# Loading the first batch's keys and queries of a head pair into one tile, keys on even and queries on odd partitions

## The chip, the core and the metric

The kernel runs on one core of a Trainium2 chip. The metric is the device time of one launch in microseconds (us), taken as the median over runs. The core has a matrix engine (PE), two elementwise engines (DVE, and ACT, which also computes the exponential), a general engine (POOL), a sequencer that mainly issues transfers (SP), and 16 DMA engines that carry all transfers between HBM and the on-chip memory.

## The reference

Attention over four batches of eight heads, and then a feed-forward layer with the maximum of three products. Heads 0, 2 and 6 see all earlier positions; the other five see the first four positions and a window of 64.

```python
scores = scale * np.matmul(q, k.transpose(0, 1, 3, 2))      # B=4, H=8, S=768, D=64
causal = rel >= 0
stream_keep = causal & (is_sink | in_win)                   # n_sink=4, window=64
scores = np.where(mask, scores, -1e9)                       # mask: causal or stream_keep, by head
a = softmax(scores)
x = np.matmul(a, v)                                         # -> rows of B*S=3072 by H*D=512
h = np.maximum(np.maximum(x @ w1, x @ w2), x @ w3)          # 512 -> 768
out = h @ w_out                                             # 768 -> 512, float32
```

Inputs are float32; the kernel computes in float16 with float32 sums.

## The kernel before

One table, `PROGRAM`, sets the order of all work: each word such as `cast 0 1 pd` calls one helper, which issues its instructions on fixed engines. Each engine runs its own instructions in that order and waits on semaphores. So nothing overtakes anything on one engine, and a late operand holds up all that stands behind it there.

Batch 0 has a path of its own, in halves of 384 positions (`HALF`), and the heads in four pairs, (0,2), (1,3), (4,6), (5,7). For each half and pair there are these steps:

- `hl half hp n ..` (`load_pairs`, DMA issues on line 206) brings the float32 keys and queries of `n` pairs from HBM. Keys go to a tile `ks`, queries to a tile `qs`, 128 partitions each. Partition p holds three consecutive rows of each head (`HB` = 3), 768 bytes that lie together in HBM. A packet is one such run. The two letters name the issuing queues for keys and queries (s is SP, c is ACT). There are 16 such loads of 192 KB in batch 0, 3.1 MB in all.
- `cast half hp ..` (`cast_pair`, line 220) makes float16 tiles `kn` and `qn`, one cast for the keys and one for the queries, each on the engine that its letter names (d DVE, a ACT, p POOL, r DVE by a reduction).
- `turnp half hp ..` (`turn_pair`, lines 238 and 241) transposes on PE into PSUM (`tr`), three 128x128 transposes for the keys and three for the queries, and copies the result into `KQ`, which holds keys and queries with the head dimension on partitions. With two letters, keys and queries are copied by two instructions, keys by the first letter's engine.
- `kx0` (lines 561 and 566) copies from the keys of `KQ` what a windowed head needs of the far block into `kx`; `s0` (lines 596, 611, 632) computes scores on PE into `st` and the exponential on ACT into `pt`.

The values come by `load_v` (line 298 in batch 0, also 768-byte runs), are cast on POOL (`vc`, line 500) and put in order by a product with a 0/1 matrix (`vt`, lines 508 and 513). From batch 1 on, keys and queries come by casting transfers that POOL issues (`load`, line 261, tile `kq`) and are turned by DVE (line 275). POOL also issues the casting loads of the weights (`w`, line 401: `w0t`, `w1t`, `w2t`). `f` is the product with a weight (line 440), `av` the product of scores and values (line 720).

The tiles of the first two loads, `ks0`, `qs0`, `ks1` and `qs1`, stand alone. The other three groups (`n` = 2, two pairs in a tile) share two buffers of the pool `pairs2`, so the third group waits until the casts have read the first. A transfer also waits for the one that last used its semaphore; eight semaphores (DMAHW0 to 7) go round among the loads of SP and ACT.

Of the kernel before, what the change touches and what calls it, by code (L numbers as in the profile page):

```python
# [9 lines left out]
FP16 = mybir.dt.float16  # L10
FP32 = mybir.dt.float32
# [5 lines left out]
PAIRS = ((0, 2), (1, 3), (4, 6), (5, 7))  # L17
# [136 lines left out]
def fast(ctx, tc, keep, q, k, v, is_retrieval, n_sink, window, moe_w1, moe_w2, moe_w3, moe_w_out, w_t, woutt, out):  # L154
    nc = tc.nc
    B, H, S, D = q.shape
    DMdl = out.shape[1]
    DF = moe_w1.shape[1]
    P = 128
# [4 lines left out]
    HALF = S // 2  # L164
    HB = HALF // P
# [9 lines left out]
    pairs2 = ctx.enter_context(tc.tile_pool(name="pairs2", bufs=2))  # L175
    once = ctx.enter_context(tc.tile_pool(name="once", bufs=1))
    third = ctx.enter_context(tc.tile_pool(name="third", bufs=2))
    half16 = ctx.enter_context(tc.tile_pool(name="half16", bufs=3))
# [11 lines left out]
    def bank(shape, dtype, name):  # L190
        return bkp.tile(shape, dtype, tag="bank", name=name)
# [4 lines left out]
    staged, cast, KQs, landed = {}, {}, {}, {}  # L196

    def load_pairs(half, hp, n, engines):
        for nm, src, eng in zip(("ks", "qs"), (k, q), engines):
            st = (  # L200
                pairs2.tile([P, 4, HB, D], FP32, tag=nm, name=nm) if n == 2
                else once.tile([P, 2 * n, HB, D], FP32, name=f"{nm}{hp}")
            )
            for h in range(0, 2 * n, 2):
                h0, h1 = PAIRS[hp + h // 2]
                eng.dma_start(
                    out=st[:, h : h + 2],
                    in_=src[0, h0 : h1 + 1 : h1 - h0, half * HALF : (half + 1) * HALF].rearrange(
                        "h (p j) d -> p h j d", p=P
                    ),  # L210
                )
            for i in range(n):
                staged.setdefault((half, hp + i), []).append(st[:, 2 * i : 2 * i + 2])
                landed[half, hp + i] = st[0:1, 2 * i, 0, 0:2]

    def cast_pair(half, hp, engines):
        cast[half, hp] = []
        for nm, src, op in zip(("kn", "qn"), staged.pop((half, hp)), engines):
            x = half16.tile([P, HB, 2, D], FP16, tag=nm, name=nm)
            op(out=x, in_=src.rearrange("p h j d -> p j h d"))  # L220
            cast[half, hp].append(x)

    def of_pair(hp):
        return KQs[0, hp // 2].rearrange("p i t two -> p i (t two)")[
            :, hp % 2
        ].rearrange("p (i t) -> p i t", i=2)

    def turn_pair(half, hp, *engines):
        if (0, hp // 2) not in KQs:
            KQs[0, hp // 2] = qkt.tile([P, 2, S, 2], FP16, tag="KQ", name="KQ")  # L230
        xs = cast.pop((half, hp))
        n = 2 // len(engines)
        for part, op in enumerate(engines):
            tr = bank([P, 1024], FP16, "tr")
            for i in range(n):
                for j in range(HB):
                    c = i * HALF + j * P
                    nc.tensor.transpose(
                        tr[:, c : c + P], xs[part + i][:, j].rearrange("p h d -> p (h d)"), ident
                    )  # L240
            op(
                out=of_pair(hp)[
                    :, part : part + n, half * HALF : (half + 1) * HALF
                ].rearrange("p i (t j) -> p i t j", j=HB),
                in_=tr[:, 0 : n * HALF].rearrange("p (i j t) -> p i t j", i=n, j=HB),
            )

    def load(b, quad, *which):
# [61 lines left out]
    def load_first(half, hp, n, e="sc"):  # L310
        by = {"s": nc.sync, "c": nc.scalar}
        load_pairs(half, hp, n, [by[x] for x in e])
# [11 lines left out]
    def idle_work(n):  # L324
# [11 lines left out]
        out=kb[:, 2:4], in_=kb[:, 2:4], compare_op=ALU.is_ge, fill=0.0,  # L336
# [3 lines left out]
        out=kb[:, 3], in_=kb[:, 3], compare_op=ALU.is_gt, fill=0.0,  # L340
# [3 lines left out]
        out=kb[:, 1:5:3], in_=kb[:, 1:5:3], compare_op=ALU.is_gt, fill=0.0,  # L344
# [7 lines left out]
        out=every3, in_=every3, compare_op=ALU.not_equal, fill=1.0,  # L352
# [4 lines left out]
    if n_sink > 0:  # L357
# [4 lines left out]
        out=far, in0=kb[:, 0:5], scalar1=FAR, scalar2=-FAR, op0=ALU.mult, op1=ALU.add  # L362
# [74 lines left out]
    def hidden(b, half, wi, ni, op=None):  # L437
        yy = psum(b, half)
        for ks in range(KS):
            nc.tensor.matmul(  # L440
                yy[:, 0:HALF],
                w_t[wi][:, ks, ni * P : (ni + 1) * P],
                xT[b, half, ks].rearrange("p a t -> p (a t)"),
                start=(ks == 0), stop=(ks == KS - 1),
            )
        if wi == 0:
            acc[b, half, ni] = accp.tile([P, HALF], FP16, tag="acc", name="acc")
            op(out=acc[b, half, ni], in_=yy[:, 0:HALF])  # L448
            return
        if wi == 2:  # L450
            hT[b, half, ni] = htp.tile([P, HALF], FP16, tag=f"hT{ni}", name=f"hT{ni}")
        nc.vector.tensor_tensor(  # L452
            out=acc[b, half, ni] if wi == 1 else hT[b, half, ni],
            in0=yy[:, 0:HALF], in1=acc[b, half, ni], op=ALU.max,
        )
# [243 lines left out]
    def masks(b, s, xy, i, engine):  # L699
        rows, (c0, step), pattern = KEEP[s][xy][i]  # L700
        mask(pts[b, s, xy], rows[0], len(rows), c0, step, pattern, engine)
# [37 lines left out]
    def turn_x(b, half, hp, op):  # L739
        x = xs.pop((b, half, hp))  # L740
        tr = bank([P, 1024], FP16, "tr")
        for i in range(HB):
            nc.tensor.transpose(
                tr[:, i * P : (i + 1) * P], x[:, i].rearrange("p h d -> p (h d)"), ident
            )
        op(out=xT[b, half, hp].rearrange("p a t -> p (a t)"), in_=tr[:, 0:HALF])
# [55 lines left out]
    def reduce_one(out, in_):  # L802
# [5 lines left out]
    engines = {"d": nc.vector, "p": nc.gpsimd}  # L808
# [5 lines left out]
        k=lambda b, s, xy, i, e: masks(int(b), int(s), xy, int(i), engines[e]),  # L814
        f=lambda b, half, wi, ni, *e: hidden(int(b), int(half), int(wi), int(ni), *[ops[x] for x in e]),
# [7 lines left out]
        x=lambda b, half, hp, e: turn_x(int(b), int(half), int(hp), ops[e]),  # L823
        turn=lambda *a: turn(*map(int, a)),
        load=lambda *a: load(*map(int, a)),
        load_v=lambda b, half, *h: load_v(int(b), int(half), queues[h[-1]], *map(int, h[:-1])),
        hl=lambda h, hp, n, *e: load_first(int(h), int(hp), int(n), *e),
        cast=lambda h, hp, e: cast_pair(int(h), int(hp), [ops[x] for x in e]),
        turnp=lambda h, hp, e: turn_pair(int(h), int(hp), *[ops[x] for x in e]),
        idle=lambda n: idle_work(int(n)),  # L830
        clear=lambda j, e: clear_v(int(j), engines[e]),
# [213 lines left out]
```

## Time and profile before

| | us |
|---|---|
| median of three runs | 189.75 |
| lowest and highest run | 189.44, 190.21 |
| span of the profiled execution, first to last instruction | 188.2 |
| PE busy in it | 178.9 (95%) |
| DVE, ACT, POOL busy | 144.1, 99.4, 83.0 |
| batch 0's transfers from SP and ACT, in the main | 2 to 17 |
| POOL's casting loads of weights and batch 1 | 16 to 40 |

The profile gives the profiled execution as a span alone; the median of the runs lies 1.55 us above it, which is taken for what lies before the first and after the last instruction. Of the rows that follow, those of the timeline begin with the start in us and the duration in us; brackets at the end give how long the engine stood idle before and what released it. The chain of work goes back from the last instruction, at each step to what released it. The DMA views count packets, megabytes and the time the packets took, as a share of all 16 DMA engines' time; a share over 100% means that packets of an engine overlap. In the table of stages, the columns behind the engines' busy times are the granted clock of PE, the busy share of the DMA engines and the rate in GB/s.

### The profile page before, as it was taken

The page shows a single profiled execution, that of the slowest core. Times are in us where ns is not written, and L with a number is a line of the kernel's source. Part 1 is how long each engine was busy: PE and PEld are TensorE (multiplying, and loading weights), DVE is VectorE, ACT ScalarE, POOL GpSimd, SP SyncE. Part 2 cuts the span into 40 slices and gives each one's busy share as a digit, 9 for nine tenths or more (in the row PEclk, how much of TensorE's full clock was granted, in tenths as well). Part 3 has the DMA queues.
Part 4 walks back from the last instruction along what each step waited for, and adds up shares of the span by engine and source line. Part 5 has one row for each costly group of instructions (what it writes and reads, how often), then busy time and mean ns, then how long its engine had stood idle before and what let it go on. Part 6 is the DMA issues. An engine that isn't in the chain of part 4 may idle for free.

```text
span 188.2 us, 4755 instructions
## 1 busy us (share of the span) xinstructions
PE 178.9 (95%) x1863; PEld 105.4 (56%) x1863; DVE 144.1 (77%) x306; ACT 99.4 (53%) x161; POOL 83.0 (44%) x142
## 2 busy tenths in 40 slices
PE   7789898999999999999999999999999999999990
PEld 2355546566566456855555556655745574664550
DVE  3749997989899978888979899756874698574540
ACT  3399996368965648687096336764445301311110
POOL 7697899808884890199057002127213400000000
PEclk9999999999999999999999999999999999999999
DMA  5999999998799999439693301321231013301413
GB/s 172 325 329 275 213 212 208 212 229 188 163 130 158 144 280 185 127 74 236 156 262 80 112 0 56 66 80 56 41 87 74 0 62 69 129 0 56 167 56 120
DMA packets 43012, 26.30 MB, mean 140 GB/s; under 512 B 29802, under 2 KB 38506, under 8 KB 42986
## 3 DMA queue, kind: packets, MB, share of 16 engines
q1 hardware_dynamic: 37562, 17.24, 35.6%
q0 software_dynamic: 4192, 7.87, 23.4%
q10 hardware_dynamic: 1232, 0.85, 1.5%
q8 instruction: 15, 0.25, 0.6%
q14 instruction: 11, 0.09, 0.1%
HBM read 25.17 MB, written 6.29 MB: 167 GB/s over the span
## 4 chain that ended last, share of the span: by engine, by line
PE 78%; DMA 13%; DVE 2%; POOL 2%; ACT 2%; issue 1%; ACTq 0%; DVEq 0%; POOLq 0%
PE yy L440 44%; PE yy L465 15%; PE st L677 7%; PE oacc L720 7%; DMA kq<-in_k_dram 7%; DMA qs<-in_q_dram 5%; PE yst L440 3%; DVE KQ L275 2%; DMA ks<-in_k_dram 2%; PE yst L465 1%; DVE acc L452 1%; POOL vx L529 1%; ACT qn L220 0%; ACT pt L632 0%; POOL w1t L401 0%
## 5 line engine op out<-in xcount | busy, mean ns | idle before, releaser
L380 POOL TENSOR_TENSOR pt<-pt,kb 128x512 f16<-128x512 f16 (+5 forms) x53 | 48.3, 931 | 59.7 <-ACT pt L694 51.1
L694 ACT ACTIVATE pt<-st 128x1024 f16<-128x1024 f32 (+2 forms) x51 | 43.5, 908 | 25.1 <-PE st L677 24.7
L440 PE MATMUL yy<-xT,w2t 128*128 128x384 f16 x184 | 36.2, 326 | 0.0
L440 PE MATMUL yy<-xT,w0t 128*128 128x384 f16 x180 | 34.8, 326 | 0.0
L440 PE MATMUL yy<-xT,w1t 128*128 128x384 f16 x176 | 34.3, 326 | 0.0
L465 PE MATMUL yy<-woutt,hT 128*128 128x512 f16 (+1 forms) x138 | 31.4, 372 | 0.0
L452 DVE TENSOR_TENSOR hT<-yy,acc 128x384 f16<-128x384 f32 x46 | 25.2, 555 | 4.6 <-PE yy L440 2.9
L452 DVE TENSOR_TENSOR acc<-yy,acc 128x384 f16<-128x384 f32 x44 | 23.9, 554 | 6.2 <-PE yy L440 4.3
L275 DVE STREAM_TRANSPOSE KQ<-kq 128x384 f32<-128x384 f32 x24 | 25.5, 1131 | 1.3 <-DMA kq<-in_k_dram 1.1
L448 ACT CAST acc<-yy 128x384 f16<-128x384 f32 x27 | 12.9, 492 | 23.5 <-PE yy L440 21.4
L440 PEld LDWEIGHTS <-w0t 128*128 128x128 f16 x192 | 18.1, 98 | 12.8 <-issue 0.7
L440 PEld LDWEIGHTS <-w1t 128*128 128x128 f16 x192 | 17.8, 98 | 12.0 <-issue 0.6
L440 PEld LDWEIGHTS <-w2t 128*128 128x128 f16 x192 | 17.7, 98 | 11.8 <-issue 0.2
L465 PEld LDWEIGHTS <-hT 128*128 128x128 f16 x150 | 14.4, 98 | 15.3
L720 PEld LDWEIGHTS <-pt 128*128 128x128 f16 x472 | 17.2, 97 | 4.2 <-DVE pt L380 0.9
L720 PE MATMUL oacc<-va,pt 128*128 128x65 f16 x392 | 18.6, 193 | 0.8 <-DVE pt L380 0.8
L474 ACT COPY ot<-yy 128x512 f32<-128x512 f32 (+1 forms) x14 | 7.9, 565 | 21.5 <-PE yy L465 18.9
L727 DVE TENSOR_TENSOR x<-oacc,sums 128x384 f16<-128x384 f32 x32 | 17.8, 557 | 1.1
L632 ACT ACTIVATE pt<-st 128x1024 f16<-128x1024 f32 (+5 forms) x22 | 15.4, 769 | 0.4 <-PE st L611 0.2
L677 PE MATMUL st<-KQ 32*128 32x128 f16 (+2 forms) x342 | 15.2, 257 | 0.1
L380 DVE TENSOR_TENSOR pt<-pt,kb 128x256 f16<-128x256 f16 (+4 forms) x31 | 12.4, 405 | 2.1 <-ACT pt L694 2.1
L677 PEld LDWEIGHTS <-KQ 32*128 32x128 f16 x342 | 8.8, 92 | 6.8 <-issue 6.0
(117 smaller groups left out, 190.5 us busy)
## 6 DMA issues: line engine op xcount, KB each, us to landing
out_dram<-ot SPq DMA_DIRECT2D x23, 256.0 KB, 2.0
vs<-in_v_dram SPq DMA_DIRECT2D x18, 256.0 KB, 4.6
ks<-in_k_dram SPq DMA_DIRECT2D x8, 192.0 KB, 3.7
kq<-in_k_dram POOLq DMA_DIRECT2D x3, 384.0 KB, 8.1
kq<-in_q_dram POOLq DMA_DIRECT2D x3, 384.0 KB, 9.6
kq<-in_k_dram POOLq DMA_DIRECT2D x3, 288.0 KB, 5.7
kq<-in_q_dram POOLq DMA_DIRECT2D x3, 288.0 KB, 7.5
qs<-in_q_dram ACTq DMA_DIRECT2D x4, 192.0 KB, 4.9
```

The costliest lines, as they stand in the source:

```text
L275: nc.vector.transpose(out=dst.rearrange("c (p j) -> c j p", j=n)[:, j0:j1], in_=src.rearrange("c (j i) -> c j i", i=R),)
L380: engine.tensor_tensor(out=x, in0=x, in1=of_blocks(kb, pattern, rows), op=ALU.mult)
L440: nc.tensor.matmul(yy[:, 0:HALF], w_t[wi][:, ks, ni * P : (ni + 1) * P], xT[b, half, ks].rearrange("p a t -> p (a t)"), start=(ks == 0), s ...
L448: op(out=acc[b, half, ni], in_=yy[:, 0:HALF])
L452: nc.vector.tensor_tensor(out=acc[b, half, ni] if wi == 1 else hT[b, half, ni], in0=yy[:, 0:HALF], in1=acc[b, half, ni], op=ALU.max,)
L465: nc.tensor.matmul(yo[:, 0:n], hT[b, half, ns][:, tb * P : (tb + 1) * P], woutt[:, ns, c : c + n], start=(ns == 0), stop=(ns == NNB - 1),)
L474: op(out=ot[:, c : c + n], in_=yo[:, 0:n])
L632: nc.scalar.activation(out=pts[0, half, hp, u][:, r0:r1, c0:c1], in_=sts[hp][:, r0:r1, c0:c1], func=AF.Exp, scale=sc,)
L677: nc.tensor.matmul(sts["XY"[g // 2]][:, g % 2, c0 : c0 + n * P], KQ[rows, 0, ki * P : (ki + 1) * P] if kind == "p" else kx[b % 2][quad][ro ...
L694: nc.scalar.activation(out=pts[b, s, xy][:, r0:r1, c0:c1], in_=st[:, r0:r1, c0:c1], func=AF.Exp, scale=sc,)
L720: nc.tensor.matmul(o[:, i, r, 0 : D + 1], at[b, h, kind, ki, qi], vv[:, 0 : D + 1], start=(n == 0), stop=(n == len(todo) - 1), skip_group_ ...
L727: nc.vector.tensor_tensor(out=x, in0=o[:, :, :, 0:D], in1=rc.unsqueeze(3).to_broadcast([P, HB, 2, D]), op=ALU.mult,)
```

## The change

Keys and queries of a pair go to one tile `kqs` of twice the row length. A load fills 64 partitions, the even ones with keys and the odd ones with queries, and each partition takes six consecutive rows of a head, 1536 bytes. The 16 loads carry 192 KB each as before, in 128 runs instead of 256. The casts no longer part keys from queries: `kqn0` takes the first three rows of all partitions and `kqn1` the last three, so each contains both. The transposes on PE keep their number and size; the copies into `KQ` now sort even and odd columns apart, and each of the two copies writes half of the keys and half of the queries. `KQ` itself has the layout it had.

```diff
--- before.py
+++ after.py
@@ -196,28 +196,28 @@
     staged, cast, KQs, landed = {}, {}, {}, {}
 
     def load_pairs(half, hp, n, engines):
-        for nm, src, eng in zip(("ks", "qs"), (k, q), engines):
-            st = (
-                pairs2.tile([P, 4, HB, D], FP32, tag=nm, name=nm) if n == 2
-                else once.tile([P, 2 * n, HB, D], FP32, name=f"{nm}{hp}")
-            )
-            for h in range(0, 2 * n, 2):
-                h0, h1 = PAIRS[hp + h // 2]
+        st = (
+            pairs2.tile([P, 4, 2 * HB, D], FP32, tag="kqs", name="kqs") if n == 2
+            else once.tile([P, 2 * n, 2 * HB, D], FP32, name=f"kqs{hp}")
+        )
+        for i in range(n):
+            h0, h1 = PAIRS[hp + i]
+            for part, (src, eng) in enumerate(zip((k, q), engines)):
                 eng.dma_start(
-                    out=st[:, h : h + 2],
+                    out=st[part:P:2, 2 * i : 2 * i + 2],
                     in_=src[0, h0 : h1 + 1 : h1 - h0, half * HALF : (half + 1) * HALF].rearrange(
-                        "h (p j) d -> p h j d", p=P
+                        "h (p j) d -> p h j d", p=64
                     ),
                 )
-            for i in range(n):
-                staged.setdefault((half, hp + i), []).append(st[:, 2 * i : 2 * i + 2])
-                landed[half, hp + i] = st[0:1, 2 * i, 0, 0:2]
+            staged[half, hp + i] = st[:, 2 * i : 2 * i + 2]
+            landed[half, hp + i] = st[0:1, 2 * i, 0, 0:2]
 
     def cast_pair(half, hp, engines):
         cast[half, hp] = []
-        for nm, src, op in zip(("kn", "qn"), staged.pop((half, hp)), engines):
-            x = half16.tile([P, HB, 2, D], FP16, tag=nm, name=nm)
-            op(out=x, in_=src.rearrange("p h j d -> p j h d"))
+        src = staged.pop((half, hp))
+        for part, op in enumerate(engines):
+            x = half16.tile([P, HB, 2, D], FP16, tag=f"kqn{part}", name=f"kqn{part}")
+            op(out=x, in_=src[:, :, part * HB : (part + 1) * HB].rearrange("p h j d -> p j h d"))
             cast[half, hp].append(x)
 
     def of_pair(hp):
@@ -239,10 +239,10 @@
                         tr[:, c : c + P], xs[part + i][:, j].rearrange("p h d -> p (h d)"), ident
                     )
             op(
-                out=of_pair(hp)[
-                    :, part : part + n, half * HALF : (half + 1) * HALF
-                ].rearrange("p i (t j) -> p i t j", j=HB),
-                in_=tr[:, 0 : n * HALF].rearrange("p (i j t) -> p i t j", i=n, j=HB),
+                out=of_pair(hp)[:, :, half * HALF : (half + 1) * HALF].rearrange(
+                    "p i (t j) -> p i t j", j=2 * HB
+                )[:, :, :, part * HB : (part + n) * HB],
+                in_=tr[:, 0 : n * HALF].rearrange("p (j t i) -> p i t j", j=n * HB, i=2),
             )
 
     def load(b, quad, *which):
```

The number of instructions on each engine is the same. The order of issue changes on SP, where both keys and queries are loaded by SP (`hl 1 0 2 ss` and `hl 1 2 2 ss`): the queue takes the pairs one after the other instead of all keys first. These are SP's loads of the second half (pairs 0 and 1, then 2 and 3, then values), before:

```order
L206 DMA ks_245<-in_k_dram 128x2x192 [waits DMAHW3_49]
L206 DMA ks_245<-in_k_dram 128x2x192 [waits DMAHW4_49]
L206 DMA qs_248<-in_q_dram 128x2x192 [waits DMAHW5_49]
L206 DMA qs_248<-in_q_dram 128x2x192 [waits DMAHW6_49]
L206 DMA ks_323<-in_k_dram 128x2x192 [waits DMAHW7_49,DVE_49,Pool_49]
L206 DMA ks_323<-in_k_dram 128x2x192 [waits DMAHW0_49]
L206 DMA qs_326<-in_q_dram 128x2x192 [waits DMAHW1_49,Activation_49]
L206 DMA qs_326<-in_q_dram 128x2x192 [waits DMAHW2_49]
L298 DMA vs_424<-in_v_dram 128x8x192 [waits DMAHW3_49]
```

and the same place now, where `kqs_319` reuses the buffer of the first half's pairs 2 and 3:

```order
L206 DMA kqs_242<-in_k_dram 64x2x384 [waits DMAHW3_49]
L206 DMA kqs_242<-in_q_dram 64x2x384 [waits DMAHW4_49]
L206 DMA kqs_242<-in_k_dram 64x2x384 [waits DMAHW5_49]
L206 DMA kqs_242<-in_q_dram 64x2x384 [waits DMAHW6_49]
L206 DMA kqs_319<-in_k_dram 64x2x384 [waits DMAHW0_49,DVE_49,DMAHW7_49,Activation_49,Pool_49]
L206 DMA kqs_319<-in_q_dram 64x2x384
L206 DMA kqs_319<-in_k_dram 64x2x384 [waits DMAHW1_49]
L206 DMA kqs_319<-in_q_dram 64x2x384 [waits DMAHW2_49]
L298 DMA vs_419<-in_v_dram 128x8x192 [waits DMAHW3_49]
```

The fifth load, the first into the reused buffer, now waits for all the casts of that buffer, ACT's among them; before, ACT's cast was waited for two loads later.

On POOL the second place is the far keys of the first half, ahead of the two casts of the values and of POOL's first load for batch 1. `KQ_253` before, and `KQ_249` now, holds pairs 2 and 3. Before:

```order
L561 COPY kx00_155<-KQ_184 128x2x64 [waits Activation_49]
L566 COPY kx00_155<-KQ_184 128x4x4
L561 COPY kx01_156<-KQ_253 128x2x64 [waits DVE_49]
L566 COPY kx01_156<-KQ_253 128x4x4
L500 CAST vn_296<-vs_203 128x768 [waits DMAHW0_49]
L500 CAST vn_296<-vs_203 128x768 [waits DMAHW2_49]
L561 COPY kx01_156<-KQ_253 128x2x64 [waits DVE_49]
```

and now:

```order
L561 COPY kx00_153<-KQ_181 128x2x64 [waits Activation_49]
L566 COPY kx00_153<-KQ_181 128x4x4
L561 COPY kx01_154<-KQ_249 128x2x64 [waits DVE_49,Activation_49]
L566 COPY kx01_154<-KQ_249 128x4x4
L500 CAST vn_292<-vs_200 128x768 [waits DMAHW1_49]
L500 CAST vn_292<-vs_200 128x768 [waits DMAHW2_49]
L561 COPY kx01_154<-KQ_249 128x2x64 [waits DVE_49,Activation_49]
```

Nothing moved here, but the far-key copies of pairs 3 and 2 wait for both copies into `KQ`, DVE's and ACT's, where DVE's alone was enough.

## The prediction

> **What bounds the kernel now.** I read the page's busy times first, then the table by stages, then PE's waits, then the chain of work.
>
> ```profile
> span 188.2 us, 4755 instructions
> PE 178.9 (95%) x1863; PEld 105.4 (56%) x1863; DVE 144.1 (77%) x306; ACT 99.4 (53%) x161; POOL 83.0 (44%) x142
> ```
> ```profile
> core 0: us, PE busy (x) PEld busy (x) DVE busy (x) ACT busy (x) POOL busy (x), PEclk, DMA share, GB/s
> 10.00:12.00 2.00, 1.48 (x15) 0.72 (x13) 1.09 (x4) 2.00 (x5) 1.79 (x4) 1.00 1.10 330
> 18.00:20.00 2.00, 1.99 (x48) 1.65 (x49) 1.99 (x5) 1.91 (x3) 2.00 (x6) 1.00 1.09 199
> 100.00:188.00 88.00, 83.74 (x765) 49.03 (x762) 60.48 (x132) 29.98 (x50) 15.87 (x22) 1.00 0.23 68
> ```
>
> PE carries the time. From 100 us on it is busy 83.7 of 88 us, and nothing of the change lies there. In the first 20 us the DMA engines are full (share 1.10) and ACT is busy without a break (2.00 of 2 us). What the change can give or take is a shift of PE's start into its long full stretch. The waits of PE limit the gain:
>
> ```profile
> PE idl L327 <- DVE warm L330: 1.3, 1, 1.3
> PE oacc L720 <- DVE pt L380: 0.8, 1, 0.8
> PE tr L238 <- ACT qn L220: 0.6, 1, 0.6
> PE st L596 <- ACT pt L632: 0.5, 2, 0.3
> PE tr L743 <- DVE x L727: 0.4, 1, 0.4
> PE vb L508 <- POOL vn L500: 0.2, 1, 0.2
> PE st L611 <- ACT pt L632: 0.2, 1, 0.2
> PE tr L238 <- POOL kn L220: 0.2, 1, 0.2
> ```
>
> Without the first, which is the launch, these are 2.9 us. More than that cannot come back. The chain shows what stands behind them:
>
> ```profile
> 3.92 4.85 DMA qs<-in_q_dram
> 8.86 0.51 ACT qn L220
> ...
> 10.19 4.92 DMA qs<-in_q_dram
> ...
> 18.42 0.70 POOL w1t L401
> ...
> 19.96 12.38 DMA kq<-in_k_dram
> ...
> 32.46 0.78 DVE KQ L275
> ...
> 37.43 0.61 PE st L677 x10
> ```
>
> Loads of queries stand in it twice, 4.85 and 4.92 us each. The first, the fourth load of ACT's queue, lands at 8.77; ACT casts it at 8.86, and PE waits the 0.6 us for that cast.
>
> **The price of a packet.** Of four stretches of the DMA view: full 768-byte loads (10 to 12 us), one 2048-byte store (104.9 to 105.9), the last stores (185 to 188.2), and the two queues side by side (4 to 6).
>
> ```profile
> DMA packets 909, 0.66 MB, mean 330 GB/s; under 512 B 51, under 2 KB 909, under 8 KB 909
> q1 hardware_dynamic: 909, 0.66, 110.2%
> ```
> ```profile
> DMA packets 98, 0.17 MB, mean 168 GB/s; under 512 B 16, under 2 KB 16, under 8 KB 98
> q1 hardware_dynamic: 98, 0.17, 44.4%
> ```
> ```profile
> q1 hardware_dynamic: 88, 0.11, 10.4%
> ```
> ```profile
> q10 hardware_dynamic: 484, 0.35, 60.6%
> q1 hardware_dynamic: 378, 0.27, 42.7%
> ```
>
> Without the 51 short ones, 858 packets of 768 bytes took 1.102 x 16 x 2 us = 35.3 us, 41 ns each. The 82 of 2048 bytes took 0.444 x 16 x 1.0 = 7.1 us, 87 ns. A line between them gives 69 ns at 1536 bytes, an estimate. The last stores bound it from above: 0.104 x 16 x 3.2 = 5.3 us over 0.11 MB, some 72 packets of 1536 bytes, 74 ns. Two old packets cost 82 ns, so a pair saves 8 to 13 ns. Each engine carries 16 loads x 16 packets = 256 old ones, 128 pairs; the overlap of 1.10 divides: 128 x 8 / 1.1 = 0.9 us to 128 x 13 / 1.1 = 1.5 us. I take 1.2 us at the last load, between a fit and a row that are equally near. Both are stores; no row shows a load of 1536 bytes, nor one on half the partitions, so below I keep nothing, and a loss, as ends. The Trainium skill, "DMA: Bandwidth & Descriptors", section "Why small descriptors are slow (HBM only)", puts the fixed cost of a packet at about 3 cycles beside one for every 32 bytes. By that, 51 cycles replace 2 x 27, a saving of 6%, and the sum would have some 0.5 us at this place instead of 1.2; the rows here show a larger fixed part.
>
> **Where the first of it is needed.** By the rows at 4 to 6 us the two queues take turns about packet by packet. ACT's first three query loads share with SP's key loads; on one engine such a round costs 32 packets x 41 / 1.1 = 1.19 us, and then 16 x (69 to 74) / 1.1 = 1.00 to 1.08. The fourth shares with SP's values, whose packets stay at 768 bytes: 1.19 again, then 8 x (69 to 74 + 41) / 1.1 = 0.80 to 0.84. Together 0.7 to 0.95 us earlier. I take 0.8: landing at 8.0 instead of 8.77.
>
> **The added waits.** A cast needs both loads now. The rows for these places:
>
> ```profile
> 7.58 0.51 POOL L220 CAST kn<-ks 128x384 f16<-128x384 f32 x1 [0.33 <-PE st L611]
> 8.21 1.88 SPq L206 DMA_DIRECT2D ks<-in_k_dram  x2
> 8.86 0.51 ACT L220 CAST qn<-qs 128x384 f16<-128x384 f32 x1 [1.56 <-DMA qs<-in_q_dram]
> 8.90 0.56 DVE L241 COPY KQ<-tr 128x384 f16<-128x384 f16 x1 [0.46 <-PE tr L238]
> 9.42 0.34 PE L238 MATMUL tr<-ident,qn 128*128 128x128 f16 x3 [0.56 <-ACT qn L220]
> 9.54 0.29 POOL L561 COPY kx<-KQ 128x128 f16<-128x128 f16 x1
> 10.45 0.86 ACT L241 COPY KQ<-tr 128x384 f16<-128x384 f16 x2
> 11.32 0.22 PE L611 MATMUL st<-KQ,kx 64*128 64x128 f16 x2
> 15.83 0.51 POOL L220 CAST qn<-qs 128x384 f16<-128x384 f32 x1 [0.59 <-DMA qs<-in_q_dram]
> 16.88 0.40 POOL L527 COPY vx<-va 64x256 f16<-64x256 f16 x1 [0.54 <-ACT va L513]
> ```
>
> - *Casts.* The path went by the queries, which land last, so a key cast that waits for them is late only where it led. For pair 3 POOL's cast moves from 7.58 to about 8.1, beside ACT's; PE's six transposes then come at 8.7 instead of, at the last, 9.42. That takes the 0.6 us wait away.
> - *Far keys on POOL.* The copy at 9.54 now needs ACT's copy of the same pair, which ends at about 10.9 before (the first of the two in 10.45 to 11.31) and 10.1 with ACT 0.8 earlier. POOL stands still some 0.6 us longer, and behind it stand two casts of values, its first batch 1 load, two casts, the `w0t` load. PE uses these far keys at 11.32, less 0.8 is 10.5; copied by 10.6. So 0.1 us at most. POOL catches up in the idle 0.59 + 0.54 us ahead of 15.83 and 16.88. POOL's loads may be issued 1 us late: of its queue, q0, the stretch from 16 to 18 us has the first packets,
>
> ```profile
> q0 software_dynamic: 101, 0.31, 78.2%
> ```
>
>   as SP's drain, so an issue that is 1 us late is taken to cost nothing.
> - *SP.* Its fifth second-half load waits for ACT's cast: 8.6 instead of 8.21. In front of it in the queue lie values and four loads of 192 KB, 768 KB or 2.4 us at 330 GB/s, so the engines do not run dry. Taking keys and queries by turns lands the first pair sooner.
> - *Copies into KQ.* Same element count, read with the same 256-byte step in PSUM, written in threes: 0.56 on DVE and about 0.5 on ACT stay, I assume; the end of the range has 0.2 us on each of four copies on the way, 0.8 us.
>
> **The sum.** ACT is busy 2.00 of 2 us at 10 and 1.91 at 18, so its start 0.8 us earlier moves exponentials, value copies and DVE's and PE's waits behind them; the second-half loads are 1.2 us earlier and don't stop it. Then POOL's casting loads, back to back from 16 to 40 us, start up to 1.2 us earlier, the load of 12.38 us with them, and DVE at 32.46. PE at 37.43 is then earlier by the smaller shift: 0.8, less 0.1 at the far keys. Against its own execution: span 188.2 - 0.7 = 187.5; with the 1.55 us around it 189.05, against the median of 189.75.
>
> **Rivals.**
> - *Swallowed.* DVE and POOL are as full as ACT at 18 to 20 us (1.99 and 2.00 of 2). If POOL's far-key delay isn't caught up, or a late engine decides the landing as before, PE meets its waits later in the same places: 189.75, give or take 0.3. For it: the wait on DVE's mask, 0.8, lies behind a full DVE. Against: DVE's work there hangs on the loads and on ACT. If the packets stay at 768 bytes it ends here too; the runs of 1536 bytes are contiguous on both sides, so I give that little.
> - *All of it.* If the wait on DVE's mask shrinks with the earlier loads too, PE gains 1.2 to 1.5: 188.4.
> - *Half the partitions cost.* A load now writes 64 partitions, four for each engine instead of eight, every second one. If two engines then write into the same part of the memory and share its rate, a packet of 69 ns takes up to 138. Against two old ones (82) that is 56 more at worst, x 128 / 1.1 = 6.5 us later at the last load; with half of the packets met, 104 ns, 2.6 us. ACT's fourth load then lands about 1.2 us late and the rest grows behind it; PE is later by about 2, 191.8. It decides from 82 ns a packet on. Nothing in this trace shows loads on half the partitions, so nothing excludes it. The Trainium skill, "SBUF — State Buffer", section "Door 1: The DMA port swizzle (why `[64,N]` ≈ `[32,N]`)", says that 64 neighbouring partitions reach only half of 16 ports; even partitions over all 128 reach all 16 by its formula, four to a port, but which engine writes which is not told for this shape. No run so far shows it.
>
> **How the numbers follow.** A difference under 0.5% (0.95 us) can't be told from no change here. Chances: the forecast 0.48 (own range 188.6 to 189.5), swallowed 0.20, all of it 0.14, half the partitions 0.18. Faster than 188.80: "all of it" with a quarter of the forecast, 0.14 + 0.12 = 0.26. Slower than 190.70: most of the last, 0.16, and 0.02 for copies that cost more, 0.18. The rest is 0.56. The range reaches from 188.3, which leaves out about 0.06, to 191.2, which leaves out about 0.13, the worse half of the last rival.
>
> **What would show it.** In the DMA view at 10 to 12 us, 69 to 74 ns a packet of 1536 bytes and a rate above 330 GB/s; over 82 ns, the last rival. ACT's cast of pair 3 at about 8.1 and PE's 0.6 us wait gone. POOL's third far-key copy at about 10.2. POOL's first casting packets before 16 us. DVE's turn of batch 1 before 32. `KQ` copies at 0.56 and 0.5. If these come out and PE's start of L677 at 37.43 doesn't move, "swallowed" is right. The prediction is wrong if a load's landing grows, or if POOL's delay reaches the value products at PE.

## The result, and the profile after

The change made the kernel slower: 191.64 us median of five runs (190.46 to 192.88) against 189.81 for before beside it (189.44 to 190.73). The ratio is 1.0114, 95% interval 1.0076 to 1.0152; the quotient of the two medians is 1.0096. The forecast was 189.05 and its range ended at 191.2. Executions far above the others of their kernel (one of 195 us, a few of 260 to 623) count in no median and no ratio here.

The profiled execution of the changed kernel is the shortest of its five, 190.46 us with a span of 188.7, so 1.76 us lie around the span; in the later runs that difference is 1.7 to 2.1 us. Before's profiled span of 188.2 belongs therefore to a run of about 190, at the upper end of its own. So the two traces are of the shortest run of the one and of one of the longer runs of the other, 0.5 us apart at their ends: they show where the start comes late, and not where the 1.8 us between the medians are lost.

The page's busy times of the changed kernel, then PE's waits:

```profile
span 188.7 us, 4764 instructions
PE 179.5 (95%) x1863; PEld 106.2 (56%) x1863; DVE 144.3 (76%) x306; ACT 100.3 (53%) x161; POOL 82.9 (44%) x142
```
```profile
PE tr L238 <- POOL kqn L220: 1.8, 1, 1.8
PE idl L327 <- DVE warm L330: 1.3, 1, 1.3
PE st L611 <- ACT pt L632: 0.5, 2, 0.2
PE tr L743 <- DVE x L727: 0.4, 1, 0.4
PE st L596 <- ACT pt L632: 0.2, 1, 0.2
PE oacc L720 <- DVE pt L380: 0.2, 1, 0.2
```

The 0.6 us wait for ACT's cast is gone, as forecast, and the wait on DVE's mask shrank from 0.8 to 0.2. But a wait of 1.8 us stands at the very first transposes, which in before waited 0.2. The waits of the two lists add up to 4.2 us before and 4.4 now. The timeline shows where it comes from. First before, SP, ACT's queue, POOL and DVE:

```profile
0.83 0.97 SPq L206 DMA_DIRECT2D ks<-in_k_dram  x2
0.83 1.03 ACTq L206 DMA_DIRECT2D qs<-in_q_dram  x2
5.07 0.50 POOL L220 CAST kn<-ks 128x384 f16<-128x384 f32 x1 [0.65 <-DMA ks<-in_k_dram]
5.37 0.55 DVE L220 CAST qn<-qs 128x384 f16<-128x384 f32 x1 [1.32 <-DMA qs<-in_q_dram]
5.62 0.34 PE L238 MATMUL tr<-ident,kn 128*128 128x128 f16 x3 [0.22 <-POOL kn L220]
```

and the changed kernel at the same places, with ACT and SP further on:

```profile
0.83 1.65 SPq L206 DMA_DIRECT2D kqs<-in_k_dram  x2
0.83 1.38 ACTq L206 DMA_DIRECT2D kqs<-in_q_dram  x2
6.98 1.07 POOL L220 CAST kqn<-kqs 128x384 f16<-128x384 f32 x2 [2.56 <-DMA kqs<-in_k_dram]
6.94 1.93 DVE L220 CAST kqn<-kqs 128x384 f16<-128x384 f32 x4 [2.88 <-DMA kqs<-in_k_dram]
7.53 1.37 PE L238 MATMUL tr<-ident,kqn 128*128 128x128 f16 x12 [1.80 <-POOL kqn L220]
9.52 0.51 ACT L220 CAST kqn<-kqs 128x384 f16<-128x384 f32 x1
9.65 0.51 POOL L220 CAST kqn<-kqs 128x384 f16<-128x384 f32 x1 [1.61 <-DMA kqs<-in_q_dram]
10.19 0.60 SPq L206 DMA_DIRECT2D kqs<-in_k_dram  x1
12.29 0.29 POOL L561 COPY kx<-KQ 128x128 f16<-128x128 f16 x1 [0.61 <-ACT KQ L241]
33.06 2.08 DVE L275 STREAM_TRANSPOSE KQ<-kq 128x384 f32<-128x384 f32 x2 [0.47 <-DMA kq<-in_k_dram]
38.23 0.63 PE L677 MATMUL st<-KQ 32*128 32x384 f16 x18
```

SP's second load, the keys of pair 1, is issued by 2.48 instead of 1.80 us: an issue of a load takes 0.60 to 0.80 us where it took 0.37 to 0.68, in the median 0.61 where it was 0.44 to 0.46. Both first casts wait for these keys. POOL casts 1.91 us and DVE 1.57 us later than before, and PE starts its transposes 1.91 us later. ACT's cast of pair 3 runs at 9.52, not at the forecast 8.1, and POOL's cast of the same pair waits for its queries until 9.65, so they land late too. POOL's far-key copy waits the forecast 0.6 us, but at 12.29; DVE turns batch 1's second part at 33.06 instead of 32.46. PE's products of L677 begin at 38.23; before, the same timeline has them from 37.03 (the chain's 37.43 is where DVE released the last ten of them).

The queues show one more thing at the start. In the first 3 us, before and after (q1 is SP's queue, q10 ACT's):

```profile
q1 hardware_dynamic: 216, 0.16, 24.5%
q10 hardware_dynamic: 82, 0.06, 6.7%
```
```profile
q10 hardware_dynamic: 79, 0.12, 17.6%
```

Before, SP's queue moves first, at 1.93 us, and ACT's at 2.41. Now ACT's moves at 2.35 and SP's not before 3.08, by the packet records. So of the 1.91 us, 1.15 are already there at the first packet of SP's queue. The traces of the whole kernels below agree without exception: where the first loads fill 128 partitions, SP's queue starts at 1.93 us and ACT's at 2.30 to 2.65 (nine kernels, before among them); where they fill 64, ACT's starts at 2.32 to 2.35 and SP's at 2.93 to 3.09 (six). What decides which queue moves first is not shown: in the loads by themselves, below, SP's was first in five of the six stages on 64 partitions.

The stages, with the columns of the prediction's table; the second fence has those of before which it did not show:

```profile
4.00:6.00 2.00, 1.73 (x6) 0.44 (x3) 0.06 (x1) 0.00 (x0) 0.42 (x1) 1.00 0.92 307
6.00:8.00 2.00, 0.47 (x6) 0.34 (x6) 1.06 (x3) 0.09 (x1) 0.96 (x2) 1.00 0.92 302
8.00:10.00 2.00, 1.88 (x17) 1.14 (x18) 1.93 (x5) 1.89 (x5) 0.39 (x2) 0.64 1.07 359
10.00:12.00 2.00, 2.00 (x17) 1.37 (x14) 0.66 (x3) 1.70 (x4) 1.68 (x6) 0.50 0.98 330
14.00:16.00 2.00, 1.75 (x24) 1.11 (x22) 0.39 (x1) 2.00 (x3) 1.99 (x6) 1.00 0.96 263
```
```profile
6.00:8.00 2.00, 1.63 (x19) 1.04 (x21) 1.94 (x5) 1.30 (x3) 0.93 (x2) 1.00 1.07 333
14.00:16.00 2.00, 2.00 (x20) 1.00 (x19) 2.00 (x5) 1.91 (x4) 1.41 (x3) 1.00 1.10 327
```

The 1536-byte packets are as short as hoped: in the records their median is 65 ns, and their mean, which is what the prediction's 41 and 69 to 74 ns are, is 71.5 at 10 to 12 us. Yet the loads carry no more: 330 GB/s at 10 to 12 us in both kernels, 302 against 333 at 6 to 8, 263 against 327 at 14 to 16. The exception is 8 to 10 us, 359 against 329, where most packets are the values' of 768 bytes. Elsewhere the packets of an engine overlapped before (share 1.07 to 1.10) and now have gaps (0.92 to 0.98). The copies into `KQ`, of 384 columns, changed too; before and after, with the mean ns of one behind the busy time:

```profile
L241 ACT COPY KQ<-tr 128x384 f16<-128x384 f16 x6 | 2.7, 488 | 2.6 <-PE tr L238 2.6
L241 DVE COPY KQ<-tr 128x384 f16<-128x384 f16 x8 | 4.2, 550 | 1.6 <-PE tr L238 1.5
```
```profile
L241 ACT COPY KQ<-tr 128x384 f16<-128x384 f16 x6 | 3.3, 595 | 4.3 <-PE tr L238 4.3
L241 DVE COPY KQ<-tr 128x384 f16<-128x384 f16 x8 | 4.5, 583 | 3.2 <-PE tr L238 3.1
```

POOL's casting loads come later as well; its queue in the stretch from 16 to 18 us:

```profile
q0 software_dynamic: 36, 0.11, 42.6%
```

Four suspects follow: the loads on half the partitions (their issue and landing), the waits for both loads, the copies, and PE's clock, which fell to 0.64 and 0.50 after the gap. The experiments take them one by one.

### The profile page after: what moved, and what is told of

The parts are those of the page before. It is cut to its first block, busy times and chain, and to the rows that moved or that the text cites. A ratio compares the mean times of both kernels' runs of the same rounds, so it can differ in the third digit from the quotient of the medians.

```text
span 188.7 us, 4764 instructions
## 1 busy us (share of the span) xinstructions
PE 179.5 (95%) x1863; PEld 106.2 (56%) x1863; DVE 144.3 (76%) x306; ACT 100.3 (53%) x161; POOL 82.9 (44%) x142
## 4 chain that ended last, share of the span: by engine, by line
PE 86%; DVE 7%; DMA 3%; ACT 1%; issue 0%; ACTq 0%
PE yy L440 47%; PE yy L465 15%; PE oacc L720 7%; PE st L677 7%; DMA kqs<-in_q_dram 3%; PE yst L440 3%; DVE KQ L241 2%; PE st L611 1%; PE yst L465 1%; DVE KQ L275 1%; PE tr L238 1%; PE st L596 1%; DVE x L727 1%; DVE vx L803 1%; PE vb L508 1%; DVE kqn L220 1%
## 5 line engine op out<-in xcount | busy, mean ns | idle before, releaser
L677 PE MATMUL st<-KQ 32*128 32x128 f16 (+2 forms) x342 | 14.9, 257 | 0.0
L448 DVE CAST acc<-yy 128x384 f16<-128x384 f32 x18 | 9.9, 559 | 3.4 <-PE yy L440 3.0
```

Source lines behind the costliest of these rows:

```text
L677: nc.tensor.matmul(sts["XY"[g // 2]][:, g % 2, c0 : c0 + n * P], KQ[rows, 0, ki * P : (ki + 1) * P] if kind == "p" else kx[b % 2][quad][ro ...
```

## The experiments

**The loads by themselves.** Nothing but the 16 loads of a batch, in the same order on SP and ACT, one form after another; between the forms DVE copies a few elements of every tile, so its wait is the time from the first issue to the last landing. No attention is computed; the output is zeros. In the first of two such kernels the stores of these zeros ran beside the first five stages.

```python
# 128 partitions, 768 B      T[:, i, part, :, 0:192]        <- "h (p j) d -> p h (j d)", p=128
# even/odd partitions, 1536  T[part:P:2, i] ... 0:384       <- "h (p j) d -> p h (j d)", p=64
# halves, 1536               T[64*part : 64*part+64, i] ... <- the same, p=64
```

> Loads alone: attention and feed-forward are left out and the output is zeros. Seven stages, each of 16 loads of 192 KB from the same two queues (keys by SP, queries by ACT), one stage after the other: old form (128 partitions, 768-byte runs), even and odd partitions with 1536-byte runs, two halves of 64 neighbouring partitions with 1536-byte runs, even and odd with 768-byte runs, halves with 768-byte runs, then the first two again. The prediction's packet price: even/odd with 1536 bytes takes 1.2 us less than the old form (about 9.5 us at 330 GB/s). Rival, memory side or HBM sets the rate whatever the packet: the two take the same within 0.3 us. Rival, half the partitions cost: even/odd takes 1 us or more longer than the old form, also with 768-byte runs; halves at least as much. Rival, issue: the rate is equal but an issue takes 0.6 us instead of 0.45, so that with two queues (8 issues each, 4.8 us) the stage is not lengthened, but its first loads are.

Measured beside the stores: 11.77 us for the old form, 13.18 for even and odd partitions, 14.82 for halves, and with 768 bytes 13.04 and 15.84. Then, undisturbed, 11.98 for the old form and 12.76 for even and odd partitions. The new form is slower, but the stores spoil the first stages, so a second kernel put them last, and took a form with 1536 bytes on all 128 partitions (whole heads) beside the others.

> Loads alone again, with nothing beside them (the stores of the zeros now come last): twice through five stages of 16 loads of 192 KB. 128 partitions with 768-byte runs (the old form), 128 partitions with 1536-byte runs (whole heads), even/odd partitions with 1536, even/odd with 768, halves with 1536. If the size of the packet sets the rate: both stages with 1536 on 128 and on even/odd partitions are 1 us shorter than the old form. If half the partitions cost: even/odd is longer than 128 partitions by 0.7 us or more at either size, and halves by some 3. If only the issue costs: even/odd with 768 bytes, issued at about 0.55 us, is longer than the old form by no more than the first load's 0.2 us.

DVE's rows in this kernel; the stages are old, whole heads, even/odd 1536, even/odd 768, halves, and then old, whole heads, even/odd 1536 again:

```profile
21.17 0.20 DVE L38 COPY sink<-T 128x64 f32<-128x64 f32 x1 [12.61 <-DMA T<-in_q_dram]
32.90 0.20 DVE L38 COPY sink<-T 128x64 f32<-128x64 f32 x1 [11.53 <-DMA T<-in_q_dram]
45.92 0.20 DVE L38 COPY sink<-T 128x64 f32<-128x64 f32 x1 [12.82 <-DMA T<-in_k_dram]
58.72 0.20 DVE L38 COPY sink<-T 128x64 f32<-128x64 f32 x1 [12.61 <-DMA T<-in_q_dram]
74.06 0.20 DVE L38 COPY sink<-T 128x64 f32<-128x64 f32 x1 [15.14 <-DMA T<-in_q_dram]
86.79 0.20 DVE L38 COPY sink<-T 128x64 f32<-128x64 f32 x1 [12.53 <-DMA T<-in_q_dram]
98.85 0.20 DVE L38 COPY sink<-T 128x64 f32<-128x64 f32 x1 [11.87 <-DMA T<-in_k_dram]
111.44 0.20 DVE L38 COPY sink<-T 128x64 f32<-128x64 f32 x1 [12.40 <-DMA T<-in_q_dram]
```

Packets of 1536 bytes do save time where a load fills 128 partitions: 11.53 and 11.87 against 12.61 and 12.53. On the even or odd partitions the saving is gone: 12.82 and 12.40. Whole heads also read one block of 192 KB in HBM instead of two of 96; so does the stage of 768 bytes on even and odd partitions, without a gain (12.61, and 12.97 the second time). Each stage ran once or twice, and the old form took 11.98 in the kernel before, so these differences are sure to about half a us. The median packet is the same in both 1536-byte forms, 65 ns (36 ns at 768 bytes), and so is the mean, 71 to 74 (38.5), so it is not the packet that grew. A part of what is missing lies at the start: by the records the first packet of a stage comes 1.44 to 1.51 us after DVE's copy on even and odd partitions, and 0.98 to 1.12 on 128. From the first to the last packet the old form takes 10.8 us twice, whole heads 10.0 and 10.4, even and odd partitions 10.9 and 10.4. And the issue of one load shows its shape; min, median and max ns, of the old form, whole heads and even/odd 1536:

```profile
L43 SPq DMA_DIRECT2D T<-in_k_dram x16: 367/376/469, 8.6 to 82.0; - x16
L64 SPq DMA_DIRECT2D T<-in_k_dram x16: 328/328/433, 21.4 to 95.0; - x16
L46 SPq DMA_DIRECT2D T<-in_k_dram x16: 601/602/798, 33.1 to 106.3; - x16
```

Halves are the worst form, 15.14 us, with a median packet of 94 ns. In the kernel they were tried as well.

**Keys on partitions 0 to 63, queries on 64 to 127.**

```diff
-                    out=st[part:P:2, 2 * i : 2 * i + 2],
+                    out=st[64 * part : 64 * part + 64, 2 * i : 2 * i + 2],
```

> The change, but keys on partitions 0 to 63 and queries on 64 to 127 instead of even and odd. If the unevenness comes from two engines meeting in one part of the memory: neighbouring partitions meet differently, so the time moves by 1 us or more against the change (slower if a load reaches half as many parts, 193 or more). If it is issue time or the waits: the same as the change within 0.6 us, 191.6.

Measured 193.3 us, ratio 1.0201 [1.0157, 1.0245], and PE's first wait grew to 2.7 us. With the size of the packets as in the change, where the partitions of a load lie sets how late PE starts.

**Waits for both loads, old loads.** Keys and queries of a pair share a tile side by side on 128 partitions, in the old runs of 768 bytes; each cast takes one head of keys and queries, so it needs both loads, and SP issues by turns.

```diff
+                    out=st[:, 2 * i : 2 * i + 2, part],
+        for c, op in enumerate(engines):
+            op(out=x[:, :, :, c], in_=src[:, c])
```

> The old runs (768 bytes, 128 partitions) with the new waits and the new order of issue: keys and queries in one tile, a cast takes one head of both, so it needs both loads. If the waits for both loads are the cause: slower than before by 1 to 2 us. If it is the form of the load (half the partitions, issue time): within 0.5 us of before, since the queries landed last already.

Measured 190.35 us, ratio 1.0043 [1.0012, 1.0073]: that lies between the two expectations. By these values the waits alone are more than a third of the loss, with an interval from a tenth to two thirds. They are not quite the waits of the change: here a transpose needs both casts of its pair, where in the change it needs one, so they may be the heavier ones.

**Keeping PE busy.** The changed kernel with 16 filler products at the start instead of 11.

```diff
-    "idle 11, hl 0 2 2 sc, cast 0 1 pd, ...
+    "idle 16, hl 0 2 2 sc, cast 0 1 pd, ...
```

> The change with 16 filler products at the start instead of 11, so that PE does not stand idle before its first transposes. If the drop of the granted clock to 0.5 to 0.64 between 8 and 12 us costs time: 0.5 to 1 us faster than the change, near 190.8. If ACT and the loads set that stretch: the same as the change within 0.4 us.

The clock came back, 1.00 in the row at 10 to 12 us where the changed kernel had 0.50:

```profile
10.00:12.00 2.00, 1.31 (x17) 0.99 (x18) 0.94 (x2) 2.00 (x4) 1.88 (x6) 1.00 0.97 341
```

The time did not: 191.58, ratio 1.0111 [1.0076, 1.0147]. PE waits for data there, at either clock.

**One part in the new form, the rest in the old.** The first two pairs of the first half come by single loads and start PE; the other six follow.

```diff
+    NEW = [(0, 0), (0, 1)]                                  # first two pairs alone
+    NEW = [(0, 2), (0, 3), (1, 0), (1, 1), (1, 2), (1, 3)]  # the other six alone
```

> The other part alone: the two single pairs at the start in the new form, all else in the old. If the start carries the loss: 1 us or more slower than before. If the second half does: within 0.5 us of before. If the parts add: this and the kernel without the first pairs together lose 2 us.

> The change without its first two pairs: the two loads of single pairs at the start are in the old form, the other six pairs of batch 0 in the new one. If the late first transposes carry the loss: within 0.4 us of before. If the loads of the second half carry it (SP alone issues them, at 0.66 us each): 1 us or more slower than before.

Measured 190.99, ratio 1.0081 [1.0044, 1.0119], for the first two pairs, and 190.88, ratio 1.0071 [1.0043, 1.0099], for the other six. Both parts cost; their sum, 1.5%, is a little over the whole, 1.1%.

**The same two parts with the waits alone**, that is with old loads on 128 partitions and a tile for both (the condition chooses the pairs). In both kernels the casts of the first two pairs write into a tile of the pool of `pt`.

```diff
+        if half == 0 and hp < 2:      # first two pairs; the complement: half == 1 or hp >= 2
```

> Before, with the loads of all pairs on 128 partitions as they were; only the first two pairs of the first half have one staging tile whose casts each read keys and queries (by head), so that each cast waits for both loads; the cast tile of these two comes from the pool of pt. Theory 1 (the form on half the partitions delays the start, the wait for both loads only a little): first transposes on PE at about 6.2 us (5.6 before, 7.5 with the new form), time 0.1 to 0.4% above before. Theory 2 (waiting for both loads is what delays the start, whatever the form): transposes at 7 us or later, 0.6 to 0.9% above before, like the run with only the first two pairs in the new form (0.8%).

> The complement: all loads on 128 partitions as before, the first two pairs of the first half wait as before, and the casts of the other six pairs each wait for keys and queries; SP issues keys and queries by turns in the second half. Theory 1 (form): within 0.3% of before; with the first two pairs' share it adds up to the 0.4% of joint waits everywhere. Theory 2 (waits): 0.5 to 0.8% above before, like the run with the other six pairs in the new form (0.7%).

Measured 189.7, ratio 1.0011 [0.9988, 1.0035], and 190.08, ratio 1.0029 [1.0004, 1.0053]. POOL's first cast in the two kernels with only the first two pairs changed, waits alone and then the new form:

```profile
5.39 0.69 POOL L241 CAST pt<-kqs 128x384 f16<-128x384 f32 x1 [0.97 <-DMA kqs<-in_q_dram]
```
```profile
6.91 0.50 POOL L248 CAST kqn<-kqs 128x384 f16<-128x384 f32 x1 [2.48 <-DMA kqs<-in_k_dram]
```

To wait for both loads costs POOL 0.3 us at the start (5.39 against 5.07) and the kernel nothing that can be told; the form of the loads costs another 1.5 us at the casts. PE's first transposes come at 6.13 with the waits alone, as the first theory says, and at 7.46 with the new form. That settles what delays the start. Of the time, the new form with its copies costs most of the 0.8%; how much of that is the copies of these two pairs was not tried.

**The order of issue alone**, keys and queries by turns in the second half, with separate tiles:

```diff
+        for i in range(n):
+            for st, src, eng in zip(tiles, (k, q), engines):
```

> Before, with only the order of issue of the change: keys and queries of a pair by turns, in the second half on one queue; separate tiles, casts that wait for one load each. If the order matters by itself, the time moves by more than 0.3%; I expect within 0.3% of before, and a gain of at most 0.3% if the first pair of the second half is cast sooner.

Measured 189.91, ratio 1.0011 [0.999, 1.0031]: nothing that can be told.

**Fewer, larger issues.** If the longer issue on SP were what holds up the loads, one load of 384 KB for two pairs would help; tried in the changed kernel and in before.

```diff
+        if n == 2:
+            eng.dma_start(out=st[part:P:2], in_=src[0, 2 * hp : 2 * hp + 4, ...])   # in before: out=st
```

> The change with one load for two pairs wherever two share a tile: 6 loads of 384 KB instead of 12 of 192 KB. If the issue time of a load is what costs: 0.5 to 1 us faster than the change, near 190.8. If the engines' uneven landing costs, or the wait for both: the same as the change or slower, since a pair now waits for its neighbour too.

> Before, with the two-pair groups loaded by one transfer of 384 KB for the keys and one for the queries, so 6 issues on SP and ACT in place of 12, packets of 768 bytes on 128 partitions as before. If the issue time of SP and ACT were what the loads wait for, this gains 0.3 to 0.6%. If the landing of a pair is what counts, a pair now waits for a load twice as large and it loses 0.3 to 0.8%; merging lost 0.5% on top of the new form. I expect the loss.

Measured 192.54, ratio 1.0162 [1.0123, 1.02], and 192.27, ratio 1.0147 [1.0113, 1.0181]. In before the loss is larger than I expected. PE's scores of pair 0 wait for DVE's copy, and that copy stands on DVE behind the cast of pair 2's keys, which waits for the joint load:

```profile
PE st L622 <- DVE KQ L252: 2.2, 1, 2.2
8.88 0.55 DVE L231 CAST kn<-ks 128x384 f16<-128x384 f32 x1 [2.16 <-DMA ks<-in_k_dram]
```

So the grain of the first loads matters more than the number of issues. This does not clear the issue time of the single loads, since merging adds a loss of its own.

**What remains of the other six pairs.** They lose 0.7%, of which the waits alone make 0.3. Three kernels split what is left: the new copies in before; the old copies in the changed kernel; and only pairs 2 and 3 of the first half in the new form. In the first two the copies do not fit the casts, so `KQ` has keys and queries mixed and batch 0's attention is not that of the reference; more than the permuted positions that were expected. The instructions keep their number and size, and only the time is used.

```diff
# new copies into KQ in before, and the reverse in the changed kernel
+                out=of_pair(hp)[:, :, half * HALF : (half + 1) * HALF].rearrange(
+                    "p i (t j) -> p i t j", j=2 * HB
+                )[:, :, :, part * HB : (part + n) * HB],
# pairs 2 and 3 of the first half
+    NEW = [(0, 2), (0, 3)]
```

> Before in its loads and casts; only the copies into KQ sort as the change does, so that each of the two writes half of the keys and half of the queries in runs of three, and the far-key copies on POOL wait for both; the positions come out permuted, the number of instructions and their sizes stay. Theory C (copies and far keys are most of the 0.4% that remain for the last six pairs beside the waits): 0.3 to 0.6% above before, ACT's copies at about 0.59 us instead of 0.48. Theory D (landing and issue of the loads on 64 partitions are): within 0.2% of before, though ACT's copies show 0.59 us all the same.

> The changed kernel with the copies into KQ of before (keys by one, queries by the other, contiguous), positions permuted. Theory C: 0.3 to 0.6% below the changed kernel, so 0.55 to 0.85% above before. Theory D: like the changed kernel, 1.0 to 1.2% above before.

> Before, with only pairs 2 and 3 of the first half in the new form (the tile taken from another pool, so that the second half's loads wait for no cast). Of the 0.7% of the six pairs: if the second half's loads, alone on SP at 0.60 us an issue, carry the form's cost, this is within 0.2% of before; if the landing of pairs 2 and 3, the far keys and ACT's copies do, it is 0.4 to 0.7% above.

The new copies in before: 189.46, ratio 0.9993 [0.9974, 1.0013], with ACT's copies as long as in the changed kernel (the trace is of an execution of 623 us, so nothing but the copies' own length is read from it):

```profile
L241 ACT COPY KQ<-tr x6: 586/590/599, 11.0 to 35.6; 128x384 f16<-128x384 f16 x6
```

The changed kernel with the old copies: 190.68, ratio 1.0052 [1.0034, 1.0071], half of the loss gone. So neither expectation held in both: the copies cost nothing where the loads come as before, and some 0.6% (1.0114 less 1.0052, measured beside different runs of before, with the intervals up to 0.4 on either side) where the loads come late. That fits copies that lie in ACT's idle time in before and on the path in the changed kernel, where ACT starts its first one at 7.91 instead of 6.00; that they are on it is argued and not shown, and which copy it is was not tried.

Pairs 2 and 3 of the first half alone: 190.77, ratio 1.006 [1.0032, 1.0087], about as much as all six. PE's waits in the trace are twice for POOL's casts:

```profile
PE tr L266 <- POOL kn L242: 0.9, 1, 0.9
PE tr L266 <- POOL kqn L248: 0.9, 1, 0.9
```

This trace is of the shortest run of its nine, 189.27 us, below before's median, so the two waits do not account for the 0.6%. By the medians the loss of the six lies in the first half; the second half's loads, eight issues of 0.60 us alone on SP, add 0.1% to it, with some 0.4 on either side.

## Why the prediction was wrong

- **The saving at the last load, the term of 1.2 us: failed.** It went from the price of a packet straight to the landing of a load. The price held: 71.5 ns in the mean, where 69 to 74 was forecast. But the loads by themselves show that nothing of it arrives on half the partitions (12.82 and 12.40 against 12.61 and 12.53: 0 where the sum had 1.2, and a loss of 0.8 in the first kernel's undisturbed stages). The same packets on 128 partitions save 0.7 to 1.1 us. The section of the Trainium skill that the prediction weighed, "DMA: Bandwidth & Descriptors", "Why small descriptors are slow (HBM only)", would put 6% there; the stages of whole heads are 5 to 9% shorter, so on 128 partitions the trace comes out near it, and on 64 the shape undoes it.
- **"Casts: the path went by the queries, which land last, so a key cast that waits for them is late only where it led": failed, by what it left out.** It was priced at pair 3 alone. At the first pair it was the keys that led: PE waited for POOL's key cast (the last row of the waits quoted there). There the wait and the new form together came to 1.9 us at PE. The waits by themselves are 0.4% over all pairs and 0.1% at the start, the second not to be told from nothing.
- **ACT's fourth load, the term of 0.8 us: failed with the first.** 9.52 instead of the forecast 8.1 for the cast, and POOL's cast of the same pair was held until 9.65 by the same load. The 0.6 us wait did go, but with all of PE later.
- **The issue of a load was not in the sum at all.** It took 0.61 us in the median against 0.44 to 0.46; at the start SP's second issue ends 0.68 us later. The start of SP's queue was not in it either: its first packet moves 1.15 us later, and no longer ahead of ACT's.
- **"An issue that is 1 us late is taken to cost nothing", "the engines do not run dry": the second failed, the first is open.** SP's fifth load of the second half was issued at 10.19, not 8.6, behind ACT's cast; the rate at 14 to 16 us is 263 against 327 GB/s, and of POOL's queue the stretch from 16 to 18 us has 36 packets where it had 101. What that costs in the end was not separated; the second half's loads as a whole add little by the last experiment.
- **Copies into `KQ`: a missed size.** 0.11 us each on ACT and 0.03 on DVE instead of nothing; the end of the range had 0.2. They cost time only together with late loads.
- **Far keys on POOL:** the forecast 0.6 us wait is there, 0.61, and no wait of PE for these copies stands in its list.
- **The rival "half the partitions cost" gave 191.8**, close to the 191.64, and its direction was right. Its mechanism was not: it was to decide from 82 ns a packet on, and the packets took 71.5, below it. What the traces show late is the issue of the loads, the start of SP's queue and the landing of the last part. The rule on neighbouring partitions in the Trainium skill, "SBUF — State Buffer", "Door 1: The DMA port swizzle (why `[64,N]` ≈ `[32,N]`)", points the same way as the halves: 94 ns a packet, 15.14 us, 2.0% slower. Even partitions, which reach every port by its formula, keep 65 ns a packet and still carry no more than before.

What stays open: why ACT's queue starts ahead of SP's when the first loads fill 64 partitions, and what delays SP's second load by the other 0.76 of 1.91 us; why the kernel's loads leave gaps between packets in some stretches; and where a run of the median, 1.2 us longer than the profiled one, loses its time.

## What to carry to other kernels

A larger packet is worth what the whole load gains, and that depends on how many partitions the load fills: measure the loads by themselves in the shape that they will have before pricing a saving. When two loads are joined into one tile, look first at the operation that starts the bound engine: a wait that is hidden behind another pair later is bare there. And a longer copy or issue that is free in one schedule can be on the path once something ahead of it is late, so price it without its cover too.

## What the runs showed of the hardware that was not expected

- The issue of a 192 KB load on SP took 0.33 us (128 partitions, 1536-byte runs), 0.38 us (128, 768), 0.55 us (64, 768) and 0.60 us (64, 1536) by the medians of the loads alone: it goes with the number of partitions more than with the number of packets, which is twice as high in the cheaper form of 768 bytes.
- Of two queues that start together, SP's moved its first packet at 1.93 us and ACT's 0.4 to 0.7 us later when the first loads filled 128 partitions; with first loads on 64 ACT's moved first, at 2.32 to 2.35, and SP's 0.6 to 0.8 us later. In the loads alone the order on 64 partitions was not always this one.
- A load on 64 neighbouring partitions has packets of 94 ns in the median where every second partition has 65, at the same size.
- PE's granted clock was 0.64 and 0.50 over 4 us after PE had been busy for 0.47 of 2 us; with fillers it stayed at 1.00, and the time was the same.
- Two loads of 192 KB joined to one of 384 made the kernel before 1.5% slower, no less than the whole change, though it issues six loads fewer.
